# A recurrent attention and routed feed-forward kernel: K's factor made on GpSimd instead of by a second triangular sum, loads issued in another order, the last steps rearranged

## The chip, the cores and the metric

The kernel runs on one core of a Trainium2 chip. A core has five engines that run their own instruction queues, each in order, and meet only by semaphores: TensorE (PE; its weight loads are listed apart as PEld), VectorE (DVE), ScalarE (ACT), GpSimd (POOL) and SyncE (SP), which here does nothing but issue DMAs. The metric is the device time of one launch in microseconds (us). The kernel before took 241.16 us, the median of three runs (240.4 to 242.75).

## The reference

First an attention with a decaying state, then a feed-forward block for 128 chosen rows of each batch. There are B = 4 batches, H = 8 heads, S = 768 steps, D = 48 channels a head, so C = H*D = 384 columns; the hidden size is F = 1024. All data are float32.

```
for t in range(S):                       # state: D x D for each batch and head
    y[t]  = r[t] . (state + (u * k[t]) v[t]^T)
    state = w[t][:, None] * state + k[t] v[t]^T

x = y as (B, S, H*D)
for each batch b:
    scores = x[b] @ w_gate
    top = the 128 rows with the highest scores
    out[b] = x[b];  out[b, top] = x[top] + sigmoid(scores[top]) * (relu(x[top] @ w1) @ w2)
```

The decay w lies between 0.8 and 0.95.

## The kernel before

**Attention in chunks.** Each batch is cut into six chunks of 128 steps, 24 chunks in all, numbered n. A chunk is held as 128 partitions (its steps) by 384 columns. The decays inside a chunk become two scaled operands: with s the sum of ln w from a step to the end of its chunk, R = r * exp(-s), and K = k * exp(s without the step's own ln w). In `sums` TensorE multiplies ln w by a triangular matrix `tri` (the step itself included) into a PSUM bank; ScalarE reads it twice, as `rise` = exp(-s) and, for one partition, as `line`, the decay over the whole chunk, which SyncE sends by DMA into `all_buf` in another layout. In `later_sums` a second product with `tri_s` (the step itself left out) fills another bank, of which ScalarE makes `e`, the factor of K. `scaled` multiplies K and R on VectorE; `turned` transposes both on TensorE, and ScalarE copies the result out (Kt, Rt). `scores` and `fresh` make the products of K with R and of K with v, four 64-row quarters a head pair, `masked` applies the causal mask, `states` carries the state on (`mid` on VectorE, and `s0` = `mid` times `all` on GpSimd), `from_state` and `from_chunk` add the two parts of y in the PSUM tiles `p_bufs`, of which there are two, and `result` adds the step's own term `vo`, makes the row's score and stores x. `vo` comes from GpSimd: `own_products` (two multiplications, `rk`), `own_sum` (VectorE), `own_values`. The first `rk` is made to wait for the second product of `scaled`.

**The feed-forward part.** `select(b)` ranks the scores of batch b (TensorE transposes, six comparisons `ahead` on VectorE, a product `ps_r`, the one-hot matrix `pick`, a product `ps_i`, the indices, an indirect gather by GpSimd, transposes of the gathered rows, the gate); `forward(b)` does the two matrix products in 16 steps, adds, and scatters the rows back with an indirect DMA. Both are generators: each `yield` ends a step, and `mix` takes steps from them by a string, "s" for select and "f" for forward.

**Order.** All instructions stand in the order in which the program writes them; nothing reorders them. The loop over n runs from -4 to 23, and in turn n it works on several chunks: `lnw(n+4)`, `from_state(n)`, `scores(n+1)`, `fresh(n+1)`, `from_chunk(n)`, `masked(n+1)`, `states(n+1)`, `result(n)`, `scaled(n+3)`, `own_products(n+3)`, `own_values(n+1)`, `own_sum(n+2)`, then steps of the feed-forward part of the batch before, `turned(n+2)`, `sums(n+4)`, more steps, `later_sums(n+4)`, more steps. Which steps go where is the table `plan`, one entry for each of the six turns of a batch; `forward(b)` starts at the fifth turn. I call these turns j = 0 to 5. In `from_state` ScalarE reads two columns (`seen`), and `from_chunk` waits for that.

**Loads.** SyncE issues everything but the indirect DMAs, in program order: 18 loads ahead of the loop, then in turn n the four tensors of chunk n+7, one piece of w1 or w2 (turns 0 to 6), the store of x, and the DMA into `all_buf`.

**PSUM.** `p_bufs` take four banks, the rotating pair psR two (`ps_x`, `ps_l` and both transposes), and psM one bank "m" (all of select) and one bank "f" (forward).

**The end.** After the loop the remaining steps run by a string, then `forward(3)`. Last, `guard` (sums that ScalarE kept beside the exponentials) is reduced and compared with a limit; every engine loads the resulting flag `wide` into a register, and a branch on it chooses a slow general path, which these inputs don't take.

Of the kernel before, what the change touches and what calls it, by code (L numbers as in the profile page):

```python
# [9 lines left out]
FP32 = mybir.dt.float32  # L10
# [3 lines left out]
AF = mybir.ActivationFunctionType  # L14
# [3 lines left out]
L = 128  # L18
# [17 lines left out]
def kernel(  # L36
# [59 lines left out]
    def load(n, names="wkrv"):  # L96
        if n >= N:
            return
        b, ci = chunks[n]
        for name in names:  # L100
            x, bufs = dict(w=(w, 5), k=(k, 6), r=(r, 6), v=(v, 9))[name]
            t = lev.tile([L, H, D], FP32, tag=name, name=name, bufs=bufs)
            src = x[b, :, ci * L:(ci + 1) * L, :].rearrange("h t d -> t h d")
            nc.sync.dma_start(out=t, in_=src)  # L104
            work[n][name] = t
# [10 lines left out]
    tri_s = consts.tile([L, L], FP32)  # L116
# [13 lines left out]
    def lnw(n):  # L130
        if 0 <= n < N:
            t = work[n]
            t["lw"] = lev.tile([L, C], FP32, tag="lw", name="lw", bufs=2)
            nc.scalar.activation(  # L134
                out=t["lw"], in_=t.pop("w").rearrange("p h d -> p (h d)"), func=AF.Ln
            )

# [8 lines left out]
    def sums(n):  # L146
        if not 0 <= n < N:
            return
        t = work[n]
        ps = psR.tile([L, 512], FP32, tag="r", name="ps_x")  # L150
        nc.tensor.matmul(ps[:, 0:C], tri, t["lw"], start=True, stop=True)  # L151
        t["rise"] = lev.tile([L, C], FP32, tag="rise", name="rise")
        nc.scalar.activation(  # L153
            out=t["rise"], in_=ps[:, 0:C], func=AF.Exp, scale=-1.0,
            accum_out=guard[:, n, 0:1],
        )
        if chunks[n][1] > 0:
            line = line_bufs[n % len(line_bufs)]
            t["all"] = all_bufs[n % len(all_bufs)]
            nc.scalar.activation(  # L160
                out=line[:, :, 0:D, :].rearrange("o q d j -> o j q d"), func=AF.Exp,
                in_=ps[0:1, 0:C].rearrange("o (j q d) -> o j q d", q=2, d=D),
            )
            nc.sync.dma_start(out=t["all"], in_=line.rearrange("o q d j -> o (q d j)"))

    def later_sums(n):
        if not 0 <= n < N:
            return
        t = work[n]
        ps = psR.tile([L, 512], FP32, tag="r", name="ps_l")  # L170
        nc.tensor.matmul(ps[:, 0:C], tri_s, t.pop("lw"), start=True, stop=True)  # L171
        t["e"] = lev.tile([L, C], FP32, tag="e", name="e")
        nc.scalar.activation(  # L173
            out=t["e"], in_=ps[:, 0:C], func=AF.Exp, accum_out=guard[:, n, 1:2]
        )
# [23 lines left out]
    def scaled(n):  # L199
# [5 lines left out]
        for to, of, by in (("K", "k", "e"), ("R", "r", "rise")):  # L205
            t["scaled"] = nc.vector.tensor_mul(  # L206
                t[to][:, :, 0:D], t[of], t.pop(by).rearrange("p (h d) -> p h d", d=D)
            )
# [231 lines left out]
    def forward(b):  # L440

        for n, rows, where, xe, xeT, gate in chosen.pop(b, ()):
            hid = mod.tile([L, NFC, L], FP32, name="hid")
            for f0 in range(0, NFC, 4):
                ps = psM.tile([L, 4, L], FP32, tag="f", name="ps_h")
# [10 lines left out]
            ps = psM.tile([L, C], FP32, tag="f", name="ps_f")  # L456
# [16 lines left out]
    def run(*steps):  # L473
# [4 lines left out]
        ("sf", "sf", "ss"), ("f", "ssf", "sf"), ("sf", "f", "s"),  # L478
        ("f", "ff", "ss"), ("f", "f", "f"), ("f", "f", "f"),
# [9 lines left out]
    AHEAD = 7  # L489

    with tc.manual_schedule():
        nc.scalar.preload_act_table_set("natural_log_exp_and_others")
        load(0, "wkr")
        load(1, "wkr")
        load(2, "w")
        nc.sync.dma_start(out=u_bc, in_=_rows(u, L))
        load(0, "v")
        load(2, "kr")
        load(3, "w")
        nc.sync.dma_start(out=wg_bc, in_=_rows(moe_w_gate, L))  # L500
        load(1, "v")
        load(3, "kr")
        load(2, "v")
        load(3, "v")
# [4 lines left out]
        nc.vector.tensor_tensor(out=tri_s, in0=col, in1=row, op=ALU.is_gt)  # L509
# [23 lines left out]
        for n in range(-4, N):  # L533
            if n > -4:
                load(n + AHEAD)
            if n >= 0 and n < len(weights):
                to, of = weights[n]
                nc.sync.dma_start(out=to, in_=of)
            lnw(n + 4)
            from_state(n)  # L540
            scores(n + 1)
            fresh(n + 1)
            from_chunk(n)
            masked(n + 1)
            states(n + 1)
            result(n)
            scaled(n + 3)
# [3 lines left out]
            parts = ("", "", "")  # L551
            if n >= NCH:
                b, j = n // NCH - 1, n % NCH
                parts = plan[j * len(plan) // NCH]
                if j == 0:
                    steps["s"] = run(steps["s"], select(b))
                if j == plan_forward:
                    steps["f"] = run(steps["f"], forward(b))
            mix(parts[0])
            turned(n + 2, "K")  # L560
            turned(n + 2, "R")
            sums(n + 4)
            mix(parts[1])
            later_sums(n + 4)
            mix(parts[2])
        steps["s"] = run(steps["s"], select(B - 1))
        mix("ssfsfsfsfsfsffsfff" + 4 * "s" + 1000 * "f")
        mix(1000 * "s")
        steps["f"] = forward(B - 1)
        mix(1000 * "f")  # L570
# [8 lines left out]
        )  # L579

# [42 lines left out]
    with tc.If(nc.values_load(wide, min_val=0, max_val=1) > 0):  # L623
# [28 lines left out]
```

## Time and profile before

| what | value |
|---|---|
| median of three runs | 241.16 us |
| the profiled execution: its time, its span | 239.45 us, 237.5 us |
| busy: PE, DVE, ACT, POOL | 187.6, 135.5, 90.5, 93.7 us |
| DMA moved | 29.37 MB, mean 124 GB/s |

The stages follow from the start of the addition that makes x (line 322) of a chunk: x of chunk 0 starts at 29.0 us, of chunk 6 at 67.3, of chunk 12 at 113.3, of chunk 18 at 159.4; the score of chunk 23 is done at 195.4 and the last addition `ye` at 229.2.

| stretch, us | what runs | PE busy | DVE busy | POOL busy | granted clock | GB/s |
|---|---|---|---|---|---|---|
| 29.0 to 67.3 | chunks 0 to 5, no feed-forward | 32.22 | 23.15 | 19.81 | 1.00 | 200 |
| 67.3 to 113.3 | chunks 6 to 11, feed-forward of batch 0 | 36.54 | 33.44 | 23.32 | 0.93 | 192 |
| 113.3 to 159.4 | chunks 12 to 17, batch 1 | 42.94 | 32.71 | 22.76 | 1.00 | 117 |
| 159.4 to 195.4 | chunks 18 to 23, batch 2 | 31.44 | 26.90 | 15.50 | 0.95 | 41 |
| 195.4 to 229.2 | rest of batch 2, all of batch 3 | 24.25 | 7.63 | 2.07 | 0.90 | 18 |

The span runs from the first to the last instruction; the time of an execution also holds what lies around it, here 1.95 us. In the views a line is a group of instructions by program line, engine, operation and tile; "busy, mean" is its busy time and the mean duration of one, and behind the bar stands the idle time of the engine just before it, with what ended that. In a timeline a row has its start, its length, and in brackets the idle time before it and what released it. "issue" is waiting that no semaphore explains. The granted clock is the share of TensorE's full clock that was passed on.

### The profile page before, as it was taken

How to read it: one execution, taken by the hardware profiler on the slowest of the kernel's cores; microseconds unless marked ns; L12 is line 12 of the kernel's file. 1: busy time of each engine (PE TensorE's matmuls, PEld its weight loads, DVE VectorE, ACT ScalarE, POOL GpSimd, SP SyncE). 2: the span in 40 equal slices, each digit the busy share in tenths (PEclk: the TensorE clock that was granted, in tenths of full speed). 3: DMA queues.
4: the chain of work that ended last, by engine and by line, in shares of the span. 5: the costliest groups of instructions: out<-in, count | busy, mean ns of one | idle time of the engine just before them, and what ended most of it. 6: DMA issues, size and time to landing. Idle time of an engine off the chain costs nothing.

```text
span 237.5 us, 8471 instructions
## 1 busy us (share of the span) xinstructions
PE 187.6 (79%) x3634; PEld 145.0 (61%) x3634; DVE 135.5 (57%) x330; ACT 90.5 (38%) x237; POOL 93.7 (39%) x113
## 2 busy tenths in 40 slices
PE   2794997699986569899999799999977987818850
PEld 1363775567765437797767567897657876408620
DVE  6262277537567977834699676546995744510010
ACT  3583453255654133446743254546510312001100
POOL 3240575554256673354534763354546400030010
PEclk9999799999999877999999999999997999976995
DMA  7999989978999999775675928101011110020000
GB/s 139 187 195 182 180 175 217 229 148 229 227 233 215 212 207 229 152 153 120 137 169 102 204 67 202 38 3 36 33 37 36 64 55 22 0 66 0 0 28 20
DMA packets 108541, 29.37 MB, mean 124 GB/s; under 512 B 103376, under 2 KB 107728, under 8 KB 108496
## 3 DMA queue, kind: packets, MB, share of 16 engines
q1 hardware_dynamic: 107984, 27.18, 52.6%
q0 software_dynamic: 512, 1.57, 2.0%
q8 instruction: 30, 0.49, 0.9%
q14 instruction: 15, 0.12, 0.2%
HBM read 23.20 MB, written 5.51 MB: 121 GB/s over the span
## 4 chain that ended last, share of the span: by engine, by line
PE 36%; DVE 18%; issue 14%; SPq 10%; ACT 7%; DMA 5%; POOL 5%; DVEq 0%; POOLq 0%; ACTq 0%
SPq L104 9%; PE ps_h L448 8%; PE ps_p L308 6%; DVE ahead L359 5%; PE ps_x L151 5%; DMA all_buf<-line_buf 4%; PE ps_f L458 3%; PE ps_p L291 3%; ACT Kt L218 3%; PE ps_p L232 3%; PE ps_t L216 3%; PE ps_l L171 2%; PE ps_p L248 2%; DVE pick L383 2%; DVE x L322 2%
## 5 line engine op out<-in xcount | busy, mean ns | idle before, releaser
L182 POOL TENSOR_TENSOR rk<-r,k 128x384 f32<-128x384 f32 x24 | 25.0, 1041 | 34.5 <-DVE r_buf L206 34.5
L308 PE MATMUL ps_p<-v,sc 64*64 64x48 f32 x768 | 30.0, 229 | 8.5 <-ACT seen L299 5.2
L218 ACT COPY Kt<-ps_t 128x512 f32<-128x512 f32 x24 | 14.0, 585 | 55.1 <-PE ps_t L216 55.1
L280 POOL TENSOR_TENSOR s<-mid,all_buf 128x192 f32<-128x192 f32 x20 | 11.4, 571 | 57.2 <-DMA all_buf<-line_buf 20.1
L308 PEld LDWEIGHTS ps_p<-v,sc 64*64 64x64 f32 x768 | 27.2, 145 | 9.8 <-ACT seen L299 6.4
L151 PE MATMUL ps_x<-lw,tri 128*128 128x384 f32 x48 | 24.2, 589 | 10.0 <-ACT lw L134 5.3
L260 DVE TENSOR_TENSOR sc<-ps_p,mask 128x512 f32<-128x512 f32 x24 | 16.5, 686 | 26.0 <-PE ps_p L248 26.0
L448 PE MATMUL ps_h<-xeT,w 128*128 128x128 f32 x192 | 28.0, 295 | 2.0 <-ACT hid L453 1.4
L448 PEld LDWEIGHTS ps_h<-xeT,w 128*128 128x128 f32 x192 | 25.8, 206 | 5.2 <-ACT hid L453 1.8
L183 POOL TENSOR_TENSOR rk<-rk,u_bc 128x384 f32<-128x384 f32 x24 | 25.0, 1040 | 3.1 <-DMA u_bc<-in_u_dram 1.3
L359 DVE SCALAR_TENSOR_TENSOR ahead<-every,score,behind 128x768 bf16<-128x768 f32 (+5 forms) x24 | 21.6, 951 | 7.6 <-ACT every L349 7.6
L458 PE MATMUL ps_f<-w,hid 128*128 128x384 f32 x64 | 24.4, 501 | 1.4 <-ACT hid L453 1.4
L322 DVE TENSOR_TENSOR x<-ps_p,vo 128x384 f32<-128x384 f32 x24 | 13.3, 553 | 17.4 <-POOL vo L197 11.4
L197 POOL TENSOR_TENSOR vo<-v,own 128x384 f32<-128x384 f32 x24 | 22.8, 950 | 0.0
L171 PE MATMUL ps_l<-lw,tri_s 128*128 128x384 f32 x48 | 21.5, 533 | 0.0
L467 POOL DMA_INDIRECT out_dram<-ye,idx x4 | 4.3, 1078 | 40.3 <-DVE total L573 19.5
L232 PE MATMUL ps_p<-Rt,Kt 48*64 48x64 f32 x768 | 17.7, 228 | 2.5 <-DVE x L322 2.5
L291 PEld LDWEIGHTS ps_p<-s,Rt 48*64 48x64 f32 x704 | 13.4, 134 | 8.8 <-issue 3.8
L151 PEld LDWEIGHTS ps_x<-lw,tri 128*128 128x128 f32 x48 | 7.9, 206 | 16.3 <-ACT Kt L218 9.8
L153 ACT ACTIVATE rise<-ps_x 128x384 f32<-128x384 f32 x24 | 11.8, 490 | 14.5 <-PE ps_x L151 14.5
L206 DVE TENSOR_TENSOR k_buf<-k,e 128x384 f32<-128x384 f32 x24 | 14.5, 602 | 4.6 <-ACT e L173 4.6
L160 ACT ACTIVATE line_buf<-ps_x 1x384 f32<-1x384 f32 x20 | 17.0, 849 | 0.0
(78 smaller groups left out, 309.6 us busy)
## 6 DMA issues: line engine op xcount, KB each, us to landing
w<-in_w_dram SPq DMA_DIRECT2D x24, 192.0 KB, 4.0
k<-in_k_dram SPq DMA_DIRECT2D x24, 192.0 KB, 4.3
r<-in_r_dram SPq DMA_DIRECT2D x24, 192.0 KB, 4.5
v<-in_v_dram SPq DMA_DIRECT2D x24, 192.0 KB, 4.1
out_dram<-x SPq DMA_DIRECT2D x24, 192.0 KB, 3.4
w<-in_moe_w_dram SPq DMA_DIRECT2D x3, 512.0 KB, 6.0
w<-in_moe_w_dram SPq DMA_DIRECT2D x4, 384.0 KB, 4.7
all_buf<-line_buf SPq DMA_DIRECT2D x20, 2.0 KB, 2.8
```

Source lines behind the costliest of these rows:

```text
L104: nc.sync.dma_start(out=t, in_=src)
L151: nc.tensor.matmul(ps[:, 0:C], tri, t["lw"], start=True, stop=True)
L171: nc.tensor.matmul(ps[:, 0:C], tri_s, t.pop("lw"), start=True, stop=True)
L182: sync(nc.gpsimd.tensor_mul(rk, t.pop("r"), t.pop("k")), t["scaled"], "one port")
L183: nc.gpsimd.tensor_mul(rk, rk, u_bc)
L197: nc.gpsimd.tensor_mul(t["vo"], t["v"], t.pop("own").to_broadcast([L, H, D]))
L218: nc.scalar.copy(out=t[name + "t"], in_=ps)
L232: nc.tensor.matmul(P[half(sub), par, j * HB:(j + 1) * HB], t["Kt"][half(par, D), j, half(sub)], t["Rt"][half(par, D), j, half(sub)], start ...
L308: nc.tensor.matmul(t["P"][half(sub), par, j * D:(j + 1) * D], t["sc"][half(sub), par, j, :], t["v"][half(sub), 2 * j + par, :], start=(sub ...
L359: nc.vector.scalar_tensor_tensor(out=ahead[:, c, lo:S], in0=every[:, lo:S], scalar=score[:, b, c:c + 1], in1=behind[:, 0:S - lo], op0=ALU. ...
L448: nc.tensor.matmul(ps[:, q, :], w1[:, dc, (f0 + q) * L:(f0 + q + 1) * L], xeT[:, dc, :], start=(dc == 0), stop=(dc == NDC - 1),)
L458: nc.tensor.matmul(ps, hid[:, fc, :], w2[:, fc, :], start=(fc == 0), stop=(fc == NFC - 1))
```

## The change

K's factor is no longer made from a second sum. `lnw` also makes `over` = exp(-ln w) = 1/w; the new `divided` multiplies k by it on GpSimd (`kw`), and `sums` makes `fall` = exp(s) beside `rise`, from the same PSUM bank. `scaled` then multiplies `kw` by `fall`. `tri_s`, `later_sums` and its product are gone. `ps_x` now lies in the bank "m" of select, not in psR.

In a turn, `from_state` now stands ahead of `lnw`, `divided(n+3)` follows them, the steps of the plan stand in two places (behind `from_chunk`, and at the end), `turned` follows the first of them, and `sums` stands behind `result`. The plan's strings are cut anew.

The loads are issued by the turn that uses them (w four chunks, k and r three, v one ahead of the turn plus four turns), with fewer buffers (k and r 5, v 6); the pieces of w1 and w2 go out in turns 2 to 8.

At the end the flag is made and loaded right behind the loop, the string orders the last gather ahead of the last part of `forward(2)`, and `forward(3)` takes its PSUM banks from the rotating pair.

```diff
--- before.py
+++ after.py
@@ -93,16 +93,22 @@
 
     work = {n: {} for n in range(N)}
 
-    def load(n, names="wkrv"):
-        if n >= N:
+    def load(name, n):
+        if not 0 <= n < N:
             return
         b, ci = chunks[n]
-        for name in names:
-            x, bufs = dict(w=(w, 5), k=(k, 6), r=(r, 6), v=(v, 9))[name]
-            t = lev.tile([L, H, D], FP32, tag=name, name=name, bufs=bufs)
-            src = x[b, :, ci * L:(ci + 1) * L, :].rearrange("h t d -> t h d")
-            nc.sync.dma_start(out=t, in_=src)
-            work[n][name] = t
+        x, bufs = dict(w=(w, 5), k=(k, 5), r=(r, 5), v=(v, 6))[name]
+        t = lev.tile([L, H, D], FP32, tag=name, name=name, bufs=bufs)
+        nc.sync.dma_start(
+            out=t, in_=x[b, :, ci * L:(ci + 1) * L, :].rearrange("h t d -> t h d")
+        )
+        work[n][name] = t
+
+    def loads(n):
+        load("w", n + 4)
+        load("k", n + 3)
+        load("r", n + 3)
+        load("v", n + 1)
 
     weights = [
         (w1[:, c], moe_w1[c * L:(c + 1) * L, :]) for c in range(NDC)
@@ -113,7 +119,6 @@
 
     ident = consts.tile([L, L], FP32)
     tri = consts.tile([L, L], FP32)
-    tri_s = consts.tile([L, L], FP32)
     mask = consts.tile([L, HB], FP32)
     ones = consts.tile([L, 1], BF16)
     ones_f = consts.tile([L, 1], FP32)
@@ -134,6 +139,8 @@
             nc.scalar.activation(
                 out=t["lw"], in_=t.pop("w").rearrange("p h d -> p (h d)"), func=AF.Ln
             )
+            t["over"] = lev.tile([L, C], FP32, tag="over", name="over", bufs=3)
+            nc.scalar.activation(out=t["over"], in_=t["lw"], func=AF.Exp, scale=-1.0)
 
     def sync(ins, on, why):
 
@@ -147,9 +154,14 @@
         if not 0 <= n < N:
             return
         t = work[n]
-        ps = psR.tile([L, 512], FP32, tag="r", name="ps_x")
-        nc.tensor.matmul(ps[:, 0:C], tri, t["lw"], start=True, stop=True)
+        lw = t.pop("lw")
+        ps = psM.tile([L, 512], FP32, tag="m", name="ps_x")
+        nc.tensor.matmul(ps[:, 0:C], tri, lw, start=True, stop=True)
+        t["fall"] = lev.tile([L, C], FP32, tag="fall", name="fall")
         t["rise"] = lev.tile([L, C], FP32, tag="rise", name="rise")
+        nc.scalar.activation(
+            out=t["fall"], in_=ps[:, 0:C], func=AF.Exp, accum_out=guard[:, n, 1:2]
+        )
         nc.scalar.activation(
             out=t["rise"], in_=ps[:, 0:C], func=AF.Exp, scale=-1.0,
             accum_out=guard[:, n, 0:1],
@@ -163,15 +175,13 @@
             )
             nc.sync.dma_start(out=t["all"], in_=line.rearrange("o q d j -> o (q d j)"))
 
-    def later_sums(n):
-        if not 0 <= n < N:
-            return
-        t = work[n]
-        ps = psR.tile([L, 512], FP32, tag="r", name="ps_l")
-        nc.tensor.matmul(ps[:, 0:C], tri_s, t.pop("lw"), start=True, stop=True)
-        t["e"] = lev.tile([L, C], FP32, tag="e", name="e")
-        nc.scalar.activation(
-            out=t["e"], in_=ps[:, 0:C], func=AF.Exp, accum_out=guard[:, n, 1:2]
+    def divided(n):
+        if not 0 <= n < N:
+            return
+        t = work[n]
+        t["kw"] = lev.tile([L, H, D], FP32, tag="kw", name="kw")
+        nc.gpsimd.tensor_mul(
+            t["kw"], t["k"], t.pop("over").rearrange("p (h d) -> p h d", d=D)
         )
 
     def own_products(n):
@@ -202,7 +212,7 @@
         t = work[n]
         t["K"] = k_bufs[n % len(k_bufs)]
         t["R"] = r_bufs[n % len(r_bufs)]
-        for to, of, by in (("K", "k", "e"), ("R", "r", "rise")):
+        for to, of, by in (("K", "kw", "fall"), ("R", "r", "rise")):
             t["scaled"] = nc.vector.tensor_mul(
                 t[to][:, :, 0:D], t[of], t.pop(by).rearrange("p (h d) -> p h d", d=D)
             )
@@ -437,12 +447,18 @@
             if len(groups) > 1:
                 yield from forward(b)
 
-    def forward(b):
+    def forward(b, more=""):
+
+        def bank():
+
+            if more:
+                return psR.tile([L, 512], FP32, tag="r", name="ps_f")
+            return psM.tile([L, 512], FP32, tag="f", name="ps_f")
 
         for n, rows, where, xe, xeT, gate in chosen.pop(b, ()):
             hid = mod.tile([L, NFC, L], FP32, name="hid")
             for f0 in range(0, NFC, 4):
-                ps = psM.tile([L, 4, L], FP32, tag="f", name="ps_h")
+                ps = bank().rearrange("p (q t) -> p q t", t=L)
                 for q in range(4):
                     for dc in range(NDC):
                         nc.tensor.matmul(
@@ -453,7 +469,7 @@
                         nc.scalar.activation(out=hid[:, f0:f0 + 4, :], in_=ps, func=AF.Relu)
                     yield
 
-            ps = psM.tile([L, C], FP32, tag="f", name="ps_f")
+            ps = bank()[:, 0:C]
             for fc in range(NFC):
                 nc.tensor.matmul(
                     ps, hid[:, fc, :], w2[:, fc, :], start=(fc == 0), stop=(fc == NFC - 1)
@@ -475,8 +491,7 @@
             yield from g
 
     plan = [
-        ("sf", "sf", "ss"), ("f", "ssf", "sf"), ("sf", "f", "s"),
-        ("f", "ff", "ss"), ("f", "f", "f"), ("f", "f", "f"),
+        ("", "fsfsss"), ("", "fssfsf"), ("", "fsf"), ("s", "fff"), ("s", "sfff"), ("", "fff")
     ]
     plan_forward = 4 * NCH // 6
     steps = dict(s=iter(()), f=iter(()))
@@ -486,27 +501,20 @@
         for x in what:
             next(steps[x], None)
 
-    AHEAD = 7
+    AHEAD = 4
 
     with tc.manual_schedule():
         nc.scalar.preload_act_table_set("natural_log_exp_and_others")
-        load(0, "wkr")
-        load(1, "wkr")
-        load(2, "w")
+        loads(-4)
+        loads(-3)
         nc.sync.dma_start(out=u_bc, in_=_rows(u, L))
-        load(0, "v")
-        load(2, "kr")
-        load(3, "w")
+        loads(-2)
+        loads(-1)
         nc.sync.dma_start(out=wg_bc, in_=_rows(moe_w_gate, L))
-        load(1, "v")
-        load(3, "kr")
-        load(2, "v")
-        load(3, "v")
 
         nc.gpsimd.iota(row, pattern=[[1, L]], base=0, channel_multiplier=0)
         nc.gpsimd.iota(col, pattern=[[0, L]], base=0, channel_multiplier=1)
         nc.vector.tensor_tensor(out=tri, in0=col, in1=row, op=ALU.is_ge)
-        nc.vector.tensor_tensor(out=tri_s, in0=col, in1=row, op=ALU.is_gt)
         nc.vector.tensor_tensor(out=ident, in0=col, in1=row, op=ALU.is_equal)
         for t in k_bufs + r_bufs:
             nc.vector.memset(t[:, :, D:HB], 0.0)
@@ -531,43 +539,36 @@
         nc.vector.tensor_copy(out=ids, in_=number)
 
         for n in range(-4, N):
-            if n > -4:
-                load(n + AHEAD)
-            if n >= 0 and n < len(weights):
-                to, of = weights[n]
+            loads(n + AHEAD)
+            if 0 <= n - 2 < len(weights):
+                to, of = weights[n - 2]
                 nc.sync.dma_start(out=to, in_=of)
+            what = ("", "")
+            if n >= NCH:
+                b, j = n // NCH - 1, n % NCH
+                what = plan[j * len(plan) // NCH]
+                if j == 0:
+                    steps["s"] = run(steps["s"], select(b))
+                if j == plan_forward:
+                    steps["f"] = run(steps["f"], forward(b))
+            from_state(n)
             lnw(n + 4)
-            from_state(n)
+            divided(n + 3)
             scores(n + 1)
             fresh(n + 1)
             from_chunk(n)
+            mix(what[0])
+            turned(n + 2, "K")
+            turned(n + 2, "R")
             masked(n + 1)
             states(n + 1)
             result(n)
+            sums(n + 4)
             scaled(n + 3)
             own_products(n + 3)
             own_values(n + 1)
             own_sum(n + 2)
-            parts = ("", "", "")
-            if n >= NCH:
-                b, j = n // NCH - 1, n % NCH
-                parts = plan[j * len(plan) // NCH]
-                if j == 0:
-                    steps["s"] = run(steps["s"], select(b))
-                if j == plan_forward:
-                    steps["f"] = run(steps["f"], forward(b))
-            mix(parts[0])
-            turned(n + 2, "K")
-            turned(n + 2, "R")
-            sums(n + 4)
-            mix(parts[1])
-            later_sums(n + 4)
-            mix(parts[2])
-        steps["s"] = run(steps["s"], select(B - 1))
-        mix("ssfsfsfsfsfsffsfff" + 4 * "s" + 1000 * "f")
-        mix(1000 * "s")
-        steps["f"] = forward(B - 1)
-        mix(1000 * "f")
+            mix(what[1])
 
         total = setup.tile([L, 1], FP32)
         nc.vector.tensor_reduce(out=total, in_=guard, axis=AX.XY, op=ALU.add)
@@ -577,6 +578,13 @@
         nc.vector.tensor_scalar(
             out=wide, in0=ps[0:1, 0:1], scalar1=LIMIT, scalar2=0.5, op0=ALU.is_le, op1=ALU.is_lt
         )
+        wide = nc.values_load(wide, min_val=0, max_val=1)
+
+        steps["s"] = run(steps["s"], select(B - 1))
+        mix("ssssfsfsfsfsfsffff" + "s")
+        mix(1000 * "f" + 1000 * "s")
+        for _ in forward(B - 1, "mr"):
+            pass
 
     def general(gen):
         u_t = gen.tile([D, H], FP32, name="u_t")
@@ -620,7 +628,7 @@
             for _ in run(select(b), forward(b)):
                 pass
 
-    with tc.If(nc.values_load(wide, min_val=0, max_val=1) > 0):
+    with tc.If(wide > 0):
         with tc.tile_pool(name="gen", bufs=1) as gen:
             general(gen)
```

## The prediction

> **What bounds the kernel now.** I read the page's busy shares first, then the groups, then the waits, then the chain, and last the timeline of one turn of each kind and of the end.
>
> ```profile
> PE 187.6 (79%) x3634; PEld 145.0 (61%) x3634; DVE 135.5 (57%) x330; ACT 90.5 (38%) x237; POOL 93.7 (39%) x113
> ...
> L182 POOL TENSOR_TENSOR rk<-r,k 128x384 f32<-128x384 f32 x24 | 25.0, 1041 | 34.5 <-DVE r_buf L206 34.5
> ...
> L171 PE MATMUL ps_l<-lw,tri_s 128*128 128x384 f32 x48 | 21.5, 533 | 0.0
> ```
>
> TensorE is busiest, and the removed product (L171) is 21.5 us of it, 0.9 a chunk. But the share is an average. In the stretch of chunks 12 to 17 TensorE is busy 42.9 of 46.1 us; in the 38.3 us of chunks 0 to 5 only 32.2. So a plain subtraction of 21.5 would be wrong, and each stage needs its own sum.
>
> ```profile
> POOL rk L182 <- DVE r_buf L206: 34.5, 18, 6.3
> DVE x L322 <- POOL vo L197: 11.4, 7, 2.3
> ```
>
> These two waits are a loop through two engines: x, score, K, R on VectorE, then two `rk` and `vo` on GpSimd, then the next x. In the timeline around 31 to 37 us it closes in 5.4 us (`rk` at 31.44 to `rk` at 36.82). It limits the turns without feed-forward steps.
>
> ```profile
> 66.05 3.87 DMA all_buf<-line_buf
> ...
> 79.02 3.08 DMA all_buf<-line_buf
> ```
>
> The chain also passes through late DMAs into `all_buf`: until about 90 us SyncE's queue is behind (chunk 6's x, ready at 67.9, is stored at 78.5) while 200 GB/s flow.
>
> **Start and chunks 0 to 5.** Ahead of the first `all_buf` DMA (issued at 22.57) SyncE now has 21 DMAs, not 22; one is 0.75 us, and x of chunk 0 waits for that DMA through `s0` and `vo`: -0.75. Then six loops. The added `kw` (128x384, SBUF by SBUF, like `rk`: 1.04) stands on GpSimd behind `vo`, while VectorE does x and score (0.57 + 0.57 = 1.14), so K need hardly wait. But the two engines hinder each other:
>
> ```profile
> 34.96 0.90 POOL L280 TENSOR_TENSOR s<-mid,all_buf 128x192 f32<-128x192 f32 x1 [0.65 <-DVE x L322]
> ...
> 35.42 0.85 DVE L206 TENSOR_TENSOR k_buf<-k,e 128x384 f32<-128x384 f32 x1
> ...
> 40.79 0.55 DVE L206 TENSOR_TENSOR k_buf<-k,e 128x384 f32<-128x384 f32 x1
> ```
>
> K takes 0.85 beside a GpSimd multiplication and 0.55 alone; `s0` 0.90 against 0.51. I add 0.3 a turn: loop 5.7. Bounds: 5.4 (`kw` hidden) and 6.4 (`kw` wholly in series). Six loops are 34.2 against 38.3 now. The 38.3 also holds two "issue" stalls of TensorE (1.08, 2.08) beside the big weight loads, and late `all_buf` DMAs. Those weights now go out two turns later, so SyncE reaches the `all_buf` DMAs of turns 3 to 6 some 4 to 6 us earlier (two weight issues of about 1.3 and one load; 1.2 MB at 200 GB/s is 6). With the chunks also earlier I keep 1.5 us of lateness: 35.7, **-2.6**.
>
> **Turns with feed-forward steps.** I walked one batch, T being the end of `from_chunk`. TensorE needs from T: transposes 0.9, `ps_x` 0.8 (so 1.8 with gaps), each f step 0.65 to 0.75, the next `from_state` to `from_chunk` 2.6. ScalarE now reads `ps_x` three times: `fall` 0.48, `rise` 0.48, `line` 0.84, done at T+3.7. VectorE needs x to `own` 2.6, mask to `mid` 1.4.
> - j=0: select's transposes now use the bank that `line` frees, so they wait till T+3.75. Now:
>
> ```profile
> 115.31 0.55 DVE L190 TENSOR_REDUCE own<-rk 128x8 f32<-128x384 f32 x1
> ...
> 117.78 1.37 DVE L359 SCALAR_TENSOR_TENSOR ahead<-every,score,behind 128x768 bf16<-128x768 f32 x1 [1.93 <-ACT every L349]
> ```
>
>   VectorE sits idle 1.9 and starts `ahead` at T+4.9 (T is 112.9). After: transposes, copy, Relu, transposes, copy end at T+6.1. Then 1.9 + 1.4: 9.2 from x to x, now 7.85.
> - j=1: VectorE's own work, 2.6 + 3.7 (`ahead`, beside GpSimd) + 1.4 = 7.7, now 7.45.
> - j=2, 3: `ps_i` no longer stands ahead of the next `scores`, where TensorE waited 1.46 for `pick`, VectorE 1.47 behind it. 7.3 and 5.3, now 8.4 and 7.7 (three f steps cost 2, the saved `ps_l` with its bank wait 0.9).
> - j=4: the scatter (1.08) and `kw` stand ahead of K: 6.7, now 7.4.
> - j=5: the Relu that frees bank "f" stands behind `fall`, `rise`, `line`; the second f step waits 1.7: 7.75, now 7.3.
> Sum 43.95 against 46.1: **-2.1** for batch 0 and again for batch 1. In the third batch `sums` runs in two turns only: j=0 costs 1.3, j=2 gives 2.2 (TensorE waited 3.23 there, and ran at granted clock 0.5 for 3.4 us afterwards), the rest 0.5: **-1.4**. ScalarE's added `over` (0.5) and `seen` ahead of `lnw` cost nothing as long as ScalarE's 4.5 us a turn stay under the turn. The smaller buffers cost nothing: a load's predecessor is read one turn before.
>
> **The end.** The flag's chain now stands between the last score and select: `total`, product, `wide` and register load (229.15 to 230.3 in the profile) behind three f steps: select starts 2.6 after the score, now 1.6. Below nothing it can't be; if each engine lost 4.1 us, as TensorE's branch at 230.4 does, it would be +3.5. Then the order pays:
>
> ```profile
> 207.64 1.03 POOL L467 DMA_INDIRECT out_dram<-ye,idx  x1 [17.75 <-DVE idx L394]
> 208.97 1.04 POOL L403 DMA_INDIRECT xe<-out_dram,idx  x1 [0.30 <-issue]
> ...
> 212.31 0.88 PE L411 MATMUL ps_x<-ident,xe 128*128 128x128 f32 x3 [5.47 <-DMA xe<-out_dram,idx]
> ...
> 213.75 5.03 PE L448 MATMUL ps_h<-xeT,w 128*128 128x128 f32 x24 [0.57 <-ACT xeT L413]
> ...
> 219.52 2.94 PE L448 MATMUL ps_h<-xeT,w 128*128 128x128 f32 x24 [0.75 <-ACT hid L453]
> ```
>
> The gather stands behind a scatter (1.3), `ps_r` and `ps_i` behind ten and six matmuls (2.8 together with it). After: transposes and copies 2.2, `ahead` 3.75, rank to index 3.2, gather to landing 3.3, so the rows land 15.1 after the score instead of 16.75: **-1.65**. The first 24 matmuls take 5.03 (granted clock 0.56) after TensorE idled 5.4 us, the next 2.94 (1.00). Four f steps (2.7) will fill that idle time; 1.3 stays, and an idle time of 1.46 at 132.2 left the clock at 1.00: -2.1. The Trainium skill ("TensorE: Matmul & The Clock Gate", Part 1) says that the clock halves after an idle window of about 3.4 us, a free-running one; by that the 2.1 is saved, or part of it if the window falls badly. Three banks remove the waits of 0.75 and 0.69 for the Relu: -1.4. The branch after `ye` no longer runs behind the flag: TensorE's 4.1 us ended at 234.55, the scatter landed at 234.21, so -0.75. End: **-5.9** (-2.4 if the register load goes wrong, -3.8 if the clock stays low, -7 at best).
>
> **Sum.** 0.75 + 2.6 + 2.1 + 2.1 + 1.4 + 5.9 = 14.9 off the profiled 239.45 gives 224.5. The median shown is 1.7 above that execution; 241.16 less 14.9 is 226.3. I say **225.5**, own range 219 to 231.
>
> **Rivals.**
> - GpSimd and VectorE in series (slower). If `kw` comes on top of VectorE's loop in every chunk, 24 x 1.04 = 25 us: 241.2 - 14.9 + 25 = 251, range 243 to 255. It decides from 0.62 us a chunk. For: comparisons `ahead` of 384 columns take 1.35 beside GpSimd, 0.62 alone (in the end). Against: K lost 0.3, not 1.04, and GpSimd idles 34.5 us for R. The Trainium skill ("SBUF — State Buffer", SBUF: two separate sides) speaks against the change: GpSimd reading SBUF and a VectorE instruction with two SBUF inputs exclude each other for the whole instruction. By it each meeting costs up to the 1.04 of `kw`, by the rows 0.3 to 0.7.
> - Only the end pays: the waits for the shared bank "m" and for the Relu (j=0, 5) eat the 0.9 a chunk. 241.2 - 5.9 = 235, range 231 to 240.
> - TensorE was the bound throughout: 21.5 + 5.9 saved: 214, range 210 to 218. Against: VectorE's idle time in chunks 12 to 14 is only 3.8 of 23.7 us.
>
> **Chances.** Forecast 0.62, only the end 0.17, in series 0.13, more 0.08. Faster and slower begin at 1% (2.4 us, about what a measurement of this kernel can tell from no change): of "only the end" 0.13 is faster, 0.04 the same. Faster 0.83, same 0.04, slower 0.13. The range 217 to 239 leaves out the slower case and most of the last one.
>
> **What would show it.** `kw` near 1.04 and K at 0.55 to 0.85; if K waits for `kw` by more than 0.3 a turn the loop step is wrong. `ahead` in j=0 should wait 3 us or more for `every`. The all_buf waits of GpSimd (20.1 us) should shrink. In the end the first 24 matmuls of `forward(3)` should take about 3 us, and 33.8 us (score to `ye`) become about 28.7. Wrong it would be made by a register load of several us, or by GpSimd falling a turn behind so that `s0` holds `from_state`.

## The result, and the profile after

The changed kernel takes **222.5 us** (median of four runs, 222.1 to 223.47) against 241.95 for the kernel before on the same occasions: a ratio of 0.921, 95% interval 0.914 to 0.927. The forecast was 225.5. Its profiled execution took 223.47 us with a span of 221.6, some 16 us off both; the sum had said 14.9. The total was right. Its parts were not, and K's factor, the change that gives this case its name, costs time instead of saving it. Ratios here and below are of the executions that were not disturbed, so they can differ a little from the quotient of the medians.

The page of the changed kernel, busy shares and groups:

```profile
PE 172.4 (78%) x3586; PEld 138.2 (62%) x3586; DVE 141.6 (64%) x329; ACT 102.2 (46%) x261; POOL 117.6 (53%) x137
...
L192 POOL TENSOR_TENSOR rk<-r,k 128x384 f32<-128x384 f32 x24 | 24.4, 1015 | 20.7 <-DVE r_buf L216 19.4
...
L183 POOL TENSOR_TENSOR kw<-k,over 128x384 f32<-128x384 f32 x24 | 24.4, 1018 | 3.0 <-DMA k<-in_k_dram 2.9
```

TensorE lost 15 us of work, GpSimd gained 24, as planned. VectorE, whose program the change hardly touches, is busy 141.6 us, six more than before. The waits of the changed kernel:

```profile
POOL s L290 <- DMA all_buf<-line_buf: 24.1, 8, 9.5
...
POOL rk L192 <- DVE r_buf L216: 19.4, 15, 1.5
...
DVE x L332 <- POOL vo L207: 14.5, 9, 2.1
```

GpSimd's slack fell from 34.5 to 19.4 us, and VectorE waits for it 3 us longer. The late DMAs into `all_buf` did not go: GpSimd's waits for them grew from 20.1 to 24.1 us, where the forecast had them shrink, and the chain still passes through two of them:

```profile
57.07 3.96 DMA all_buf<-line_buf
...
77.96 3.75 DMA all_buf<-line_buf
```

By stages, cut at the same events as before (x of chunks 0, 6, 12 and 18, the last score, the last addition); the columns are length, busy time of PE, PEld, DVE, ACT and POOL, granted clock, DMA share, GB/s:

```profile
27.90:64.50 36.60, 27.74 (x802) 22.62 (x802) 24.21 (x53) 21.82 (x60) 25.65 (x30) 1.00 0.85 182
64.50:107.20 42.70, 34.32 (x824) 29.78 (x825) 34.44 (x76) 20.84 (x55) 29.84 (x32) 0.84 0.88 201
107.20:152.50 45.30, 39.24 (x899) 32.65 (x897) 36.64 (x78) 25.57 (x65) 28.90 (x31) 0.96 0.69 151
152.50:189.80 37.30, 31.35 (x683) 24.96 (x680) 26.82 (x65) 12.28 (x31) 17.87 (x19) 0.91 0.12 40
189.80:216.60 26.80, 22.09 (x142) 15.70 (x142) 7.91 (x29) 3.58 (x8) 2.13 (x2) 1.00 0.08 25
```

| stage | before, us | after, us | difference | predicted |
|---|---|---|---|---|
| to x of chunk 0 | 29.0 | 27.9 | -1.1 | -0.75 |
| chunks 0 to 5 | 38.3 | 36.6 | -1.7 | -2.6 |
| chunks 6 to 11 | 46.0 | 42.7 | -3.3 | -2.1 |
| chunks 12 to 17 | 46.1 | 45.3 | -0.8 | -2.1 |
| chunk 18 to the last score | 36.0 | 37.3 | +1.3 | -1.4 |
| last score to last addition | 33.8 | 26.8 | -7.0 | -5.15 |
| from there to the end | 8.3 | 5.0 | -3.3 | -0.75 |

So the loop gave 5.6 us where 9.0 was forecast, and the end 10.3 where 5.9 was. Two errors of opposite sign met, and that they nearly cancel is luck.

### The profile page after: what moved, and what is told of

It is laid out like the page before. It is cut to its first block, busy times and chain, and to the rows that moved or that the text cites. A ratio compares the mean times of both kernels' runs of the same rounds, so it can differ in the third digit from the quotient of the medians.

```text
span 221.6 us, 8505 instructions
## 1 busy us (share of the span) xinstructions
PE 172.4 (78%) x3586; PEld 138.2 (62%) x3586; DVE 141.6 (64%) x329; ACT 102.2 (46%) x261; POOL 117.6 (53%) x137
## 4 chain that ended last, share of the span: by engine, by line
PE 27%; DVE 21%; issue 13%; POOL 11%; DMA 9%; ACT 9%; SPq 8%; POOLq 0%; DVEq 0%; ACTq 0%
SPq L102 6%; DMA all_buf<-line_buf 5%; PE ps_p L318 5%; PE ps_f L464 5%; DVE ahead L369 5%; PE ps_t L226 5%; POOL rk L192 3%; DVE scr L338 3%; POOL vo L207 3%; DVE x L332 3%; PE ps_f L474 3%; POOL rk L193 2%; DVE k_buf L216 2%; DMA xe<-out_dram,idx 2%; PE ps_p L242 2%
## 5 line engine op out<-in xcount | busy, mean ns | idle before, releaser
L192 POOL TENSOR_TENSOR rk<-r,k 128x384 f32<-128x384 f32 x24 | 24.4, 1015 | 20.7 <-DVE r_buf L216 19.4
L290 POOL TENSOR_TENSOR s<-mid,all_buf 128x192 f32<-128x192 f32 x20 | 12.2, 610 | 38.7 <-DMA all_buf<-line_buf 24.1
L369 DVE SCALAR_TENSOR_TENSOR ahead<-every,score,behind 128x768 bf16<-128x768 f32 (+5 forms) x24 | 23.4, 1024 | 8.2 <-ACT every L359 8.2
L464 PE MATMUL ps_f<-xeT,w 128*128 128x128 f32 x192 | 24.5, 278 | 4.5 <-ACT hid L469 3.9
L464 PEld LDWEIGHTS ps_f<-xeT,w 128*128 128x128 f32 x192 | 23.1, 192 | 7.5 <-ACT hid L469 4.5
L183 POOL TENSOR_TENSOR kw<-k,over 128x384 f32<-128x384 f32 x24 | 24.4, 1018 | 3.0 <-DMA k<-in_k_dram 2.9
L474 PE MATMUL ps_f<-w,hid 128*128 128x384 f32 x64 | 25.3, 529 | 0.7 <-ACT hid L469 0.7
L242 PEld LDWEIGHTS ps_p<-Rt,Kt 48*64 48x64 f32 x768 | 15.0, 141 | 7.3 <-ACT over L143 2.0
L226 PE MATMUL ps_t<-ident,k_buf 128*128 128x128 f32 x96 | 18.7, 327 | 0.0
L301 PE MATMUL ps_p<-s,Rt 48*64 48x48 f32 x704 | 16.4, 223 | 2.5 <-DVE mid L288 2.5
L474 PEld LDWEIGHTS ps_f<-w,hid 128*128 128x128 f32 x64 | 12.6, 208 | 8.0 <-issue 1.8
L226 PE MATMUL ps_t<-ident,r_buf 128*128 128x128 f32 x96 | 17.2, 310 | 0.0
```

Of the source, the lines that this page charges most:

```text
L183: nc.gpsimd.tensor_mul(t["kw"], t["k"], t.pop("over").rearrange("p (h d) -> p h d", d=D))
L192: sync(nc.gpsimd.tensor_mul(rk, t.pop("r"), t.pop("k")), t["scaled"], "one port")
L226: nc.tensor.transpose(ps[:, j, :], t[name][:, 2 * j:2 * j + 2, :], ident)
L242: nc.tensor.matmul(P[half(sub), par, j * HB:(j + 1) * HB], t["Kt"][half(par, D), j, half(sub)], t["Rt"][half(par, D), j, half(sub)], start ...
L301: nc.tensor.matmul(t["P"][half(sub), par, j * D:(j + 1) * D], t["Rt"][half(par, D), j, half(sub)], t["s1" if sub else "s0"][half(par, D), ...
L369: nc.vector.scalar_tensor_tensor(out=ahead[:, c, lo:S], in0=every[:, lo:S], scalar=score[:, b, c:c + 1], in1=behind[:, 0:S - lo], op0=ALU. ...
```

## Experiments

The change holds three separable things beside K's factor: the order of a turn, the loads, the end. The runs do each alone, undo K's factor, and then take kw apart. Medians of one kernel move by a few us from one set of runs to another, so I compare ratios to the kernel before, which ran in each set.

### The end alone

In the kernel before:

```diff
+        total, ps_w, wide = ...            # the flag's chain, from the last lines
+        wide = nc.values_load(wide, min_val=0, max_val=1)
         steps["s"] = run(steps["s"], select(B - 1))
-        mix("ssfsfsfsfsfsffsfff" + 4 * "s" + 1000 * "f")
-        mix(1000 * "s")
-        steps["f"] = forward(B - 1)
-        mix(1000 * "f")
+        mix("ssssfsfsfsfsfsffff" + "s")
+        mix(1000 * "f" + 1000 * "s")
+        for _ in forward(B - 1, "mr"):
+            pass
```

> The kernel before with the new end alone: the flag made and loaded right behind the loop, the new string of steps, forward(3) in the rotating pair of banks. Loop, loads and K's factor stay as before. In the profile of the changed kernel the stretch from the last score to the end lost 10.3 us (42.1 to 31.8). Theory (the end is independent of the rest): 241.9 - 10.3 = 231.7 us, between 229.5 and 234. Rival (the end gains only because the loop leaves TensorE less behind): 236 to 240 us.

Measured 230.34 us, 0.9585 of before (0.952 to 0.965): 10.0 us. In its profile the last score to the end takes 32.2 us, in the changed kernel 31.8. The end is independent of the loop, and by itself it gives about half of the 19 us.

### The loads alone

```diff
-    def load(n, names="wkrv"):        # bufs w 5, k 6, r 6, v 9
+    def load(name, n):                # bufs w 5, k 5, r 5, v 6
+    def loads(n):                     # w n+4, k n+3, r n+3, v n+1
...
-                load(n + AHEAD)       # AHEAD = 7; weights in turns 0 to 6
+            loads(n + AHEAD)          # AHEAD = 4; weights in turns 2 to 8
```

> The kernel before with the new order of loads, its buffers and the later weights alone. Theory: x of chunk 0 comes 1.1 us earlier and two of the late DMAs into all_buf come in time: 3 to 4 us less, 238.5 us, between 236.5 and 240.5. Rival (SyncE is held by the smaller buffers of k and r): 242 to 246 us.

Measured 236.31 us, 0.977 (0.968 to 0.987): 3.8 us by the medians, 5.5 by the ratio. That is a gain, as the theory said, but these few executions don't fix its size. x of chunk 0 starts at 26.9 us, not 29.0, and chunks 0 to 5 take 36.0 us, not 38.3. That is all of the gain of the first stages (the changed kernel gained 1.1 and 1.7 there), and K's factor has no part in it.

### K's factor undone

In the changed kernel `tri_s` and the second product are back, `over` and `divided` are gone:

```diff
-            t["over"] = exp(-lw)
-            divided(n + 3)
             sums(n + 4)
+            later_sums(n + 4)         # tri_s, in the rotating pair; fall = exp of it
...
-        for to, of, by in (("K", "kw", "fall"), ("R", "r", "rise")):
+        for to, of, by in (("K", "k", "fall"), ("R", "r", "rise")):
```

> The changed kernel with K's factor made as before: the second triangular product is back (in the rotating pair, right behind the first), the product with 1/w on GpSimd and 1/w itself are gone. Everything else of the change stays. Theory (most of what TensorE saves is lost again because GpSimd and VectorE keep each other from SBUF): 2 to 6 us more than the changed kernel, 226.5 us, between 224 and 229. Rival (TensorE bounds the loop): 0.65 to 0.9 us for each of 24 chunks, 238 to 244 us. A second rival (the factor on GpSimd costs more than it saves): 218 to 222 us.

Measured **216.31 us**, 0.901 (0.893 to 0.909). The second rival had the sign, and the gain is larger than its 218 to 222 us: the kernel is faster with TensorE's second product than without. My revised theory, that the factor still gains a little, fell here. The stages of this kernel, in the same columns:

```profile
27.60:62.10 34.50, 31.57 (x814) 25.48 (x814) 22.84 (x54) 19.71 (x53) 19.98 (x23) 0.95 0.93 196
62.10:106.00 43.90, 35.22 (x838) 29.76 (x835) 31.58 (x76) 18.18 (x49) 22.33 (x24) 0.92 0.91 206
106.00:148.70 42.70, 41.06 (x910) 33.53 (x909) 33.22 (x78) 22.54 (x59) 22.91 (x25) 1.00 0.66 146
148.70:181.50 32.80, 29.49 (x686) 23.91 (x684) 25.51 (x65) 11.62 (x30) 15.76 (x17) 1.00 0.14 45
181.50:208.30 26.80, 22.09 (x142) 15.70 (x142) 7.89 (x27) 3.54 (x8) 2.14 (x2) 1.00 0.08 25
```

In chunks 12 to 17 TensorE works 41.1 of 42.7 us, 1.8 more than in the changed kernel, and the stage is still 2.6 us shorter; VectorE works 33.2 us instead of 36.6. From chunk 18 to the last score the difference is 4.5 us; 2.9 of it is one turn in which TensorE's granted clock fell to 0.50 in the profile of the changed kernel, which is taken up further down.

### The changed kernel again

> The changed kernel itself, unchanged, to stand beside the others on one chip: 0.92 of the kernel before, 221 to 223 us. The kernel with two sums ran at 0.901; if that difference is real, this one comes at 0.915 to 0.927 again.

Measured 220.75 us, 0.920 (0.910 to 0.930). The 0.019 between it and the kernel with two sums, 4.6 us, is therefore not a matter of the occasion: the intervals, 0.893 to 0.909 and 0.910 to 0.930, don't overlap.

### The order of a turn alone

The kernel before with the new places of `from_state`, `turned` and `sums` (in the bank "m", `later_sums` behind it) and the new plan; K's factor, loads and end as before:

```diff
+            from_state(n)
             lnw(n + 4)
-            from_state(n)
...
             from_chunk(n)
+            mix(what[0])
+            turned(n + 2, "K")
+            turned(n + 2, "R")
             masked(n + 1)
             states(n + 1)
             result(n)
+            sums(n + 4)
+            later_sums(n + 4)
```

> The kernel before with the new order of a turn alone: from_state ahead of ln w, the transposes ahead of result, both triangular sums behind result (the first in select's bank), the plan's new strings. K's factor, loads and the end stay as before. The kernel with two sums (order, loads and end new) stood at 0.901 of before; the end alone took 9.7 us off, the loads alone about 4. Theory (the parts add): the order is worth the rest, 9 to 10 us, 231 us, between 228.5 and 233. Rival (order and loads need each other, since either alone leaves SyncE or TensorE late): 235 to 240 us.

Measured 232.39 us, 0.949 (0.943 to 0.955): 12.3 us of this set's 244.7, more than the 9 to 10 expected; this set runs some 4 us slower as a whole, so its ratio says more than its place in the range. The parts add, roughly: 0.0415 for the end, 0.023 for the loads and 0.051 for the order make 0.115 (28 us), and the kernel with all three stands at 0.099. From x to x the six turns of chunks 12 to 17 take 8.0, 7.4, 6.8, 5.3, 7.2 and 7.9 us; before they took 7.8, 7.4, 8.4, 7.7, 7.4 and 7.3. The gain lies in j=2 and 3, where the prediction saw it (7.3 and 5.3), and the second product is still there.

### What kw costs

In the changed kernel K is made from k, once without kw and once with a fill of GpSimd's own in its place:

```diff
-        nc.gpsimd.tensor_mul(t["kw"], t["k"], t.pop("over")...)
+        t.pop("over")                          # no_kw
+        nc.gpsimd.memset(filler, 0.0)          # kw_memset: this too, 128x1072
...
-        for to, of, by in (("K", "kw", "fall"), ("R", "r", "rise")):
+        for to, of, by in (("K", "k", "fall"), ("R", "r", "rise")):
```

> The changed kernel without the multiplication by 1/w on GpSimd: K is made from k itself, so K lacks the factor 1/w; 1/w is still computed on ScalarE. It measures what kw costs. Theory (it costs through the shared port and the loop of GpSimd and VectorE, more than the 0.3 us a chunk of the prediction): 6 to 10 us less than the changed kernel, 214.5 us, between 212 and 217. Prediction's own price: 0.3 us a chunk, 7 us at most, less where TensorE bounds: 216 to 219 us. Rival (hidden): 221 to 223 us.

Measured 215.19 us, 0.897 (0.889 to 0.906): 5.5 us below the changed kernel by the medians of the two sets. It also has no second product, and is only 1.1 us faster than the kernel that has it, within the intervals. So TensorE's 21.5 us were worth about one, not clear of nothing, and kw costs 5.5 us here and 7.5 by the ratio of the second set below.

> The changed kernel with GpSimd's multiplication kw replaced by a fill of a buffer that nothing reads, 128x1072 elements, about as long (1.04 us, reckoned from 0.62 for 128x640); K lacks the factor 1/w. The fill keeps GpSimd's queue as long as kw does but reads nothing from SBUF. Theory (kw costs because GpSimd and VectorE exclude each other from SBUF reads): near the kernel without kw, 0.897 of before, 214 to 217 us, and the time that VectorE's instructions take beyond the shortest of their shape stays near 14 us, as without kw (21 with kw). Rival (kw costs because it delays what stands behind it in GpSimd's queue): near the changed kernel, 219 to 222 us.

Measured 218.26 us, 0.914 (0.904 to 0.924), in one set with the changed kernel at 0.920. That tells nothing apart. Both again, with more executions:

> The kernel without kw once more, K without 1/w, to stand on one chip beside the one with the fill: 0.897 of before again, 214 to 217 us.

> The kernel with the fill in the place of kw once more; at three rounds it stood at 0.914, between the kernel without kw (0.897) and the changed one (0.920), with wide intervals. Theory (the port alone): within 1.5 us of the kernel without kw. Rival (the queue alone): within 1.5 us of the changed kernel, 219 to 222 us. If both count, between: 217 to 219 us.

Measured 217.43 us, 0.889 (0.884 to 0.894), without kw, and 218.11 us, 0.894 (0.888 to 0.899), with the fill. The fill took 0.99 us each, kw 1.02. So a GpSimd instruction of the same length that reads nothing costs about 1 us in all (the intervals overlap), while kw, in two other sets, puts the kernel at 0.920. One stage of the profiles tells them apart better than the medians, since it repeats within 0.3 us from profile to profile of one kernel: chunks 12 to 17 take 45.3, 45.0 and 45.0 us in the three profiles with kw (the changed kernel twice, and once with the flag late, below), 42.0 and 42.0 without it, and 42.4 and 42.4 with the fill. There kw costs 3.0 to 3.3 us and the fill 0.4. The fill also takes away that K has to wait for kw, but that isn't the cost: in the profile of the changed kernel K waited for kw once, for 3.1 us (until 10.9), ahead of the first x. So most of kw's cost comes from reading SBUF, not from the place in the queue.

The trace shows how. VectorE and GpSimd of the changed kernel, in a turn j=4:

```profile
141.90 0.84 DVE L433 SCALAR_TENSOR_TENSOR neg<-own 128x1 f32<-128x1 f32 x1
...
143.56 0.92 DVE L444 TENSOR_TENSOR gate<-gate,den 128x1 f32<-128x1 f32 x1
```

```profile
141.51 1.20 POOL L193 TENSOR_TENSOR rk<-rk,u_bc 128x384 f32<-128x384 f32 x1
...
143.47 0.99 POOL L183 TENSOR_TENSOR kw<-k,over 128x384 f32<-128x384 f32 x1
```

Instructions on one element a partition take 0.16 us alone, and here 0.84 and 0.92. They end at 142.74 and 144.48; the GpSimd instructions that ran beside them end at 142.71 and 144.46. VectorE waits until GpSimd is done. `neg` meets `rk` and takes 0.84 in the kernel without kw too; `gate` is what kw adds. The same `gate` beside the fill takes 0.16:

```profile
138.29 0.99 POOL L184 MEMSET filler<- 128x1072 f32 x1
...
138.40 0.16 DVE L443 TENSOR_TENSOR gate<-gate,den 128x1 f32<-128x1 f32 x1
```

That is what the Trainium skill says ("SBUF — State Buffer", SBUF: two separate sides): a VectorE instruction with two SBUF inputs and a GpSimd instruction that reads SBUF have the shared ports in turns, each for its whole length. Taking for each VectorE instruction the time beyond the shortest of its shape, I find 15.4 us in all before, 21.4 in the changed kernel, 14.2 without kw and 15.8 and 13.6 in the two profiles with the fill.

### The flag at the very end again

```diff
-        total, ps_w, wide = ...; wide = nc.values_load(...)     # behind the loop
         steps["s"] = run(steps["s"], select(B - 1))
...
+        total, ps_w, wide = ...                                 # behind forward(3)
+    with tc.If(nc.values_load(wide, ...) > 0):
```

> The changed kernel with the flag's chain and its load back at the very end, all else as changed. Theory (the gain between the last addition and the end, 8.3 to 5.0 us, is the flag's: its chain, the branch behind it and the landing of the scatter beside the branch's instruction fetch): +3.3 at the end, -1.0 ahead of select, 2.3 us more than the changed kernel. The prediction's price: +0.75 and -1.0, so 0.3 less than the changed kernel. Rival (the scatter landed late by chance): 0 to +0.8 us.

Measured 223.45 us, 0.926 (0.911 to 0.942), against 220.75 in the same set: the medians are 2.7 us apart, the intervals overlap. The profiles say more. From the last addition to the end this kernel takes 7.85 us, the changed one 4.96, the kernel before 8.27. The landing of the last scatter, in the lists of DMA issues near the end, first of the changed kernel and then of this one (last column: us from issue to landing):

```profile
out_dram<-ye,idx POOLq DMA_INDIRECT x1, 2.6
```

```profile
out_dram<-ye,idx POOLq DMA_INDIRECT x1, 4.4
```

Before it was 4.7. It isn't chance: in the four profiles with the flag late (before, loads alone, order alone, this one) the last scatter lands after 4.4 to 4.7 us and the stretch from the last addition to the end takes 7.85 to 8.4; in the ten with it early it lands after 2.6 to 2.9 and the stretch takes 4.9 to 5.4. With the flag late, the branches of all engines start beside the scatter, and the instruction queues move six packets of 8 KB and two of 16 KB near the end; with the flag early it is three of 8 KB. That these packets hold up the scatter fits these profiles but wasn't tried by itself.

### The second f step of j=5

In the kernel with two sums:

```diff
-        ..., ("s", "sfff"), ("", "fff")
+        ..., ("s", "sfff"), ("f", "ff")
```

> The kernel with two sums and the rest of the change, and the plan's last entry as (f, ff) instead of (none, fff): the Relu that frees bank f comes ahead of the copies and exponentials on ScalarE. Theory (the second f step of j=5 waits 1.6 us for that Relu behind the exponentials, and TensorE bounds that turn): 1 to 1.5 us less in each of three turns, 212.5 us, between 211 and 214.5. Rival (VectorE's and GpSimd's loop bounds the turn, the wait is slack): 215 to 217.5 us.

Measured 216.04 us, 0.903 (0.892 to 0.915): no difference to the kernel with two sums in the median. Its turns j=5 are shorter (6.7, not 7.9 to 8.0 us), so here it is again, with more executions:

> Two sums and the plan's last entry as (f, ff) once more; at three rounds its median was that of the kernel with two sums, though turn j=5 shrank from 8.0 to 6.7 us in its profile. Theory (the Relu's wait is on the path): 0.885 to 0.895 of before. Rival (slack): 0.898 to 0.905.

Measured **215.97 us**, 0.885 (0.880 to 0.890). That is below the changed kernel's interval and just below that of the kernel with two sums, but the median in us is the same as in the first set; between the two versions with two sums I call the time open. In the profiles chunks 12 to 17 take 41.5 and 41.6 us with the new entry and 42.7 with the old one, so the Relu's wait was on the path in those turns. Either version beats both kernels of this case: 216 us.

## Why the prediction was right in the sum and wrong in its parts

**Start and chunks 0 to 5** (-0.75, -2.6; measured -1.1, -1.7). The bound was sound. The loop through VectorE and GpSimd closes in 5.6 us in the changed kernel and 5.1 to 5.4 without kw, so 5.7 was near. The gain is the loads'. The late DMAs kept more than the 1.5 us I left them.

**The turns with feed-forward steps** (-2.1, -2.1, -1.4; measured -3.3, -0.8, +1.3). This is the step that failed. In chunks 12 to 17 the walk said 9.2, 7.7, 7.3, 5.3, 6.7, 7.75; measured were 9.1, 8.1, 6.9, 6.3, 8.1, 6.9. Two waits were read rightly. In j=0 `ahead` waits for select's transposes behind `line`:

```profile
154.80 0.83 ACT L172 ACTIVATE line_buf<-ps_x 1x384 f32<-1x384 f32 x1
...
155.68 0.54 PE L356 MATMUL ps_e<-ident,score 128*128 128x128 f32 x3 [1.19 <-ACT line_buf L172]
...
157.93 1.43 DVE L369 SCALAR_TENSOR_TENSOR ahead<-every,score,behind 128x768 bf16<-128x768 f32 x1 [2.83 <-ACT every L359]
```

and in j=5 the second f step waits 1.6 us for the Relu, predicted 1.7. The mis-sized term is kw's price in these turns. The 0.3 a turn stood in the loop of chunks 0 to 5, mostly as K's loss; here the walk named kw in j=4 alone, and left `ahead`, the score and the gate where they were. Without kw the six turns take 8.4, 7.4, 6.9, 5.1, 6.6 and 7.6, so kw costs 3.2 us in this batch alone. Turn by turn it is seen where: in j=0 the first comparison takes 1.68 us instead of 1.02, in j=1 all comparisons 4.4 instead of 3.7, in j=4 the score's product 1.26 instead of 0.56 and `gate` 0.92 instead of 0.16. The rows that would have shown it were in the trace before; I took the mean of what K lost instead of asking when each VectorE instruction meets GpSimd. The rule weighed in the rival's sentence was the right measure, of single meetings if not of every one: 24 x 1.04 did not come, because GpSimd's new time lies partly beside instructions that read only one SBUF operand (ten of the 24 kw ran beside the addition of x, which kept its 0.55 us) and partly at the tail of a meeting (nine score products lost 0.2 us).

In j=3 of this batch a second cost came on top, the clock. kw makes VectorE late for `pick`, and TensorE waits for it; first the changed kernel, then without kw:

```profile
129.55 0.32 PE L400 MATMUL ps_i<-ids,pick 128*128 128x2 bf16 x6 [2.42 <-DVE pick L393]
```

```profile
125.57 0.30 PE L397 MATMUL ps_i<-ids,pick 128*128 128x2 bf16 x6 [1.15 <-DVE pick L390]
```

In chunks 12 to 17 of the three profiles with kw this wait is 2.26 to 2.42 us, and the granted clock falls to 0.50 for 3.4 us within 1.3 us of its end; in the four without kw or with the fill it is 1.14 or 1.15, and the clock stays at 1.00. The turn takes 6.1 to 6.4 us with kw and 5.1 to 5.5 without.

In the third batch the same wait is 2.41 or 2.42 us with kw, without it and with the fill, so there it isn't kw's. Whether the clock falls around its end differs from profile to profile: it did in five of these seven, and not in two. Turn j=3, first in the changed kernel, then in the same kernel with the flag late, where the clock stayed up:

```profile
174.61 0.32 PE L400 MATMUL ps_i<-ids,pick 128*128 128x2 bf16 x6 [2.42 <-DVE pick L393]
...
176.53 4.05 PE L474 MATMUL ps_f<-w,hid 128*128 128x384 f32 x6
```

```profile
175.97 0.30 PE L400 MATMUL ps_i<-ids,pick 128*128 128x2 bf16 x6 [2.41 <-DVE pick L393]
...
177.04 2.10 PE L474 MATMUL ps_f<-w,hid 128*128 128x384 f32 x6
```

In the first the granted clock is 0.50 from 173.9 to 180.7, the six matmuls take twice as long and the turn 6.9 us; in the second the turn takes 4.0 us and the whole stage 34.4, which is 1.6 less than before, near the -1.4 of the forecast. So the +1.3 of the table is this fall of the clock. I had forecast that the wait of 3.23 us in this batch goes; it only shrank to 2.42.

**The end** (-5.15, -0.75; measured -7.0, -3.3). The flag's chain delayed select by 2.7 us after the score, as said (2.6). The gathered rows were used 14.3 us after it (15.1), because `ps_r` starts on the first comparisons while the last still run. The clock stayed up, as forecast: all 48 matmuls of `forward(3)` ran in one piece. One wait of 1.46 us that left the clock alone was thin ground for that, since behind a wait of the same length at 132.5 in the run with the end alone the clock did fall (0.50 from 135.1).

```profile
200.75 1.05 POOL L413 DMA_INDIRECT xe<-out_dram,idx  x1 [17.33 <-DVE idx L404]
...
204.09 0.52 PE L421 MATMUL ps_x<-ident,xe 128*128 128x128 f32 x3 [1.18 <-DMA xe<-out_dram,idx]
...
205.17 5.62 PE L464 MATMUL ps_f<-xeT,w 128*128 128x128 f32 x48
```

The term that was too small is the last: -0.75 for the branch that no longer runs behind the flag. I took the scatter's landing at 4.7 us as fixed; it is 2.6 when no branch runs beside it, and SyncE's closing waits end 1.1 us after that landing instead of the 2.3 with the flag late.

**The rivals.** "Only the end pays" described the split best: the end is 10 of the 16 us in the profiles. But its reason (shared bank, Relu) was not the cause, since the order of the turn with the same waits gains 12 us by itself. "In series" named the right mechanism at several times its price. That TensorE was the bound throughout is refuted: taking its second product away is worth about 1 us, within the intervals, once kw is left out as well.

## What to carry to other kernels

Before moving work to an idle engine, look at what it shares with the engine that will be next to bind: slack on GpSimd is of little use where a multiplication there stops VectorE. Price the parts of a mixed change one by one, and ask of a gain which of them it belongs to; here the order of the queues, the loads and the end would have gained some 24 us with K's factor left alone. And a branch or flag at the end of a program can cost the last DMA time: make the decision early.

## What the runs showed of the hardware

- A VectorE instruction on 128x1 with two SBUF operands takes 0.16 us alone and up to 0.92 beside a GpSimd multiplication of 128x384; it ends within 0.03 us of it. A fill on GpSimd of the same length doesn't do that: the same instruction beside it takes 0.16, and nine score products beside fills kept their 0.56.
- The length of a single wait of TensorE did not decide whether its clock falls. It stayed at 1.00 behind waits of 2.41 us (without kw, 165.2 to 167.6; flag late, 173.6 to 176.0) and fell to 0.50 within 1.2 us of the end of waits of 1.79 (order alone, 172.1 to 173.9), 1.46 (end alone, 132.5 to 134.0) and 1.30 (second f step, repeated, 165.9 to 167.2). The halves last 3.4 us or 6.8 or 10.2.
- The last indirect scatter of 128 rows lands in 2.6 to 2.9 us in the ten profiles with the flag early, and in 4.4 to 4.7 us in the four where the engines' branches run at the same time.
